# Two activations of a two-layer feed-forward kernel: parametric relu and mish as ScalarE table functions read from PSUM

## The chip, the cores and the metric

The kernel runs on one core of one Trainium2 chip. The metric is the device time of one execution in microseconds (us). Three runs of the kernel before took 880.09, 880.59 and 880.71 us; the median is 880.59.

## The reference

Packed attention (a small set of 32 queries per head draws from keys and values, and the full queries then draw from that set) is followed by two feed-forward layers. 2304 tokens (4 batches of 576), width 512, hidden width 2048, all in float32; the weights arrive as 64-bit floats.

```
x = attention(q, k, v, p)            # [2304, 512]
h = x @ w_in                         # first layer, [2304, 2048]
g = maximum(0.01 * h, h)             # leaky relu
x = g @ w_out                        # [2304, 512]
h = x @ w_in2                        # second layer
sp = where(h > 20, h, log1p(exp(minimum(h, 20))))
g = h * tanh(sp)                     # mish
out = g @ w_out2
```

## The kernel before

Products of this size carry each float32 operand as two parts: a high part, the value rounded to the type float32r, and a low part, the value less its high part. A product is then three matmuls, high x high, high x low and low x high (`PASSES`, line 20). So every block that goes into a matmul has to be made twice: rounded, and as a remainder.

**Weights** come in as 64-bit words. For each unit of 128 x 512, `convs` (line 115) puts together the float32 on VectorE in three instructions (L128, L130, L132), rounds it on ScalarE (L140) and subtracts on GpSimd (L141). The loads are issued on SyncE's queue (SP), each when the unit before it has freed its staging tile.

**First layer.** The hidden width is worked through in chunks of 128 columns, for one half batch (288 tokens, `HALF`) at a time: 128 steps, listed in `slots`. The first product is folded with the attention: `packed_w` (line 355) multiplies the packed values into the weights once for each batch and 512 columns, and ScalarE and VectorE split the result (L366, L367). A step's `l1_h` (line 373) has six matmuls of 288 columns into one of two PSUM banks of the pool `psh`, and then four instructions make the leaky relu and its two parts: a copy out of PSUM on ScalarE (L391), the relu on VectorE in place (L392), the rounding cast on ScalarE (L394), the subtraction on GpSimd (L395). `l1_y` (line 405) multiplies such a block with the output weights, twelve matmuls of 288 columns into four banks of the pool `psy` that hold a running sum over several steps. Its block is that of three steps before (`LAG`, line 663). When a sum ends, each of its four banks is copied into `yp` by ScalarE (L424) or added to it by VectorE (L426), and the next sum's first matmuls need these banks. `y_parts` (line 432) later splits the finished `yp` for the second layer (L439 on ScalarE, L441 on GpSimd).

**Attention and order.** The attention of the batches runs among these steps: `pack` and `spread` are generators that transpose, multiply, take Exps and split, and each `tick()` (line 535) advances some of them by a step. For the first layer the order of all of this is a string written out by hand (`SCHED`, line 25): each tick takes the next field and advances what its letters name (2 and 5 the attention, c the weight conversions, P the packed weights). After the string is used up, generators advance by fixed periods. Each engine works through its instructions in the order in which they were emitted.

**Second layer.** Blocks of 384 tokens (`TB`), 96 steps in the loop at line 688. `l2_h` (line 446) has twelve matmuls of 384 columns into one of three banks. `l2_g` (line 459) computes h * a / (a + 2) with a = e * (e + 2) and e = exp(min(h, 20)): VectorE clips (L463), ScalarE takes Exp (L464), VectorE makes a (L476), ScalarE takes Ln(a + 2) and the Exp of its negative (L478, L479), and in the next pass of the loop VectorE multiplies twice (L468, L469, which reads PSUM again), ScalarE rounds (L471) and GpSimd subtracts (L472). `two_c` holds the constant 2 that Ln adds. `l2_o` (line 484) takes the block of three steps before: nine matmuls of 512 columns into three banks of the pool `pso` (five banks), summed over four steps, then copied into `op` by ScalarE (L498) or added by VectorE (L500), and stored. At the start of the kernel one table set is loaded into ScalarE (L582, `natural_log_exp_and_others`).

Of the kernel before, what the change touches and what calls it, by code (L numbers as in the profile page):

```python
# [8 lines left out]
F32 = mybir.dt.float32  # L9
F32R = mybir.dt.float32r  # L10
U32 = mybir.dt.uint32
I64 = mybir.dt.int64
AF = mybir.ActivationFunctionType
ALU = mybir.AluOpType
AX = mybir.AxisListType
PSUM = bass.MemoryType.PSUM

# The large products carry a float32 operand as two float32r parts, hi = round(x)
# to 12 significant bits and lo = x - hi, and take hi*hi + hi*lo + lo*hi.
PASSES = ((0, 0), (0, 1), (1, 0))  # L20

# The order of emission: in which the first steps of the first layer's attention (0, 1, 2: pack; 3, 4, 5: spread), its packed
# queries (p), its loads and their regrouping, the first weights (C: a unit, c: a step) and products (P) start.
ORDER = "xwLPxPk0K0p01xP0x1cc0x11wxCcxxx0xxxQ1qxccw4PaC311cx3Pc40PcC4b3dcc0c31CxC40xPxxCPx13x33c3c2444c2423x34wC43x542x3x5xx434"
# [5 lines left out]
def tile_packed_attention_moe2(ctx: ExitStack, tc: tile.TileContext, q, k, v, p, w1i, w1o, w2i, w2o, out):  # L30
    nc = tc.nc
    B, H, S, D = q.shape
    NP = p.shape[2]
    NT, DM = out.shape
    DF = w1i.shape[1]
    R = 6
# [4 lines left out]
    TB = 384  # L41
# [6 lines left out]
    const = ctx.enter_context(tc.tile_pool(name="const", bufs=1))  # L48
# [3 lines left out]
    ident = const.tile([128, 128], F32, name="ident")  # L52
    two_c = const.tile([128, 1], F32, name="two_c")
    ppT = const.tile([128, B * NG, 2, 2 * NP], F32, name="ppT")
# [6 lines left out]

# [1 line left out]
    wi, wo, w2a, w2b = {}, {}, {}, {}  # L63
    w_tiles = {}

    def w_tile(kind, n):
        """The tile that the n-th group of a weight lies in, taken from the ring when first asked for."""
        if (kind, n) not in w_tiles:
            if kind == "i":
                t = wp.tile([128, 4, 512], F32, tag="A", name=f"wi{n}")  # L70
            elif kind == "o":
                t = wp.tile([128, 2, 2, 512], F32R, tag="A" if n % 4 == 2 else "B", name=f"wo{n}")
            else:
                t = wp.tile([128, 2, 2, 512], F32R, tag="A" if kind == "a" else "B", name=f"w2{kind}{n}")
            w_tiles[kind, n] = t
        return w_tiles[kind, n]
# [29 lines left out]
    def w_ahead(i):  # L106
        """Load the next unit of the weights, if it is not more than the stages allow ahead of unit i."""
        n = len(w_list_done)
        if n < len(w_list) and n <= i + (EARLY - 1 if n < 2 * EARLY else 1):
            sts[n] = w_load(w_list[n][1], n)  # L110
            w_list_done.append(n)
# [39 lines left out]

# [1 line left out]
    a2_t = {}  # L153
    packed, ready = set(), set()
# [45 lines left out]
    def spare(nm):  # L200
        """Room that the first layer's blocks take later."""
        return gp.tile([128, S], F32, tag="gx", name=nm, bufs=4)
# [10 lines left out]
    def pack(u, bank, first=False):  # L213
        """The packed queries of four heads of a batch, and the values that they draw."""
        if u == 1:
# [5 lines left out]
        if not first:  # L221
            load(k, "k", u + 1)
        # scores of the packed queries: [4 heads x NP, S]
        sc = []
        mx2 = att.tile([128, 2], F32, tag="mx2", name="mx2")
        for hb in range(2):
            ps = bank()
# [25 lines left out]
        for hb in range(2):  # L253
            ps = bank()
# [4 lines left out]
            yield  # L259
        # packed values, transposed: [2 heads x D, 4 heads x NP], the diagonal blocks kept  # L260
        ps = bank()
# [20 lines left out]
    def spread(u, bank, first=False):  # L282
        """The queries' attention over the packed keys; the first batch's in finer steps."""
        b, g = divmod(u, NG)
# [5 lines left out]
        while u not in packed:  # L290
            yield
        # scores of the queries on the packed keys, transposed: [4 heads x NP, S]
        bt = att.tile([128, S], F32, tag="sm", name="bt")
        for hb in range(2):
            ps = bank()
# [41 lines left out]

    # steps of the first layer: (pass, batch, half, chunk of 128 columns, first and last of its sum, sum's number in the pass,
    # last sum of the pass); a pass's first and last weights are used up in two sums, which leaves more time to replace them
    slots = []  # L340
# [30 lines left out]

# [1 line left out]
    def l1_h(i):  # L373
        pas, b, hb, f = slots[i][:4]
        pw = pw_t[(pas * B + b) * 2 + f % 8 // 4]
        fc = f % 4 * 128
        ps = psh.tile([128, 512], F32, tag="h", name="ps_h1")[:, :HALF]
        n = 0
        for g in range(NG):
            for x, y in PASSES:  # L380
                mm(  # L381
                    ps,
                    pw[:, g, x, fc : fc + 128],
                    a2_t[b, g][:, y, hb * HALF : (hb + 1) * HALF],
                    start=n == 0,
                    stop=n == 3 * NG - 1,
                )
                n += 1
        prog["h"] = i
        gf = gp.tile([128, HALF], F32, tag="gf", name="gf", bufs=3)  # L390
        nc.scalar.copy(gf, ps)  # L391
        nc.vector.scalar_tensor_tensor(out=gf, in0=gf, scalar=0.01, in1=gf, op0=ALU.mult, op1=ALU.max)  # L392
        gx = gp.tile([128, 2, HALF], F32R, tag="gx", name="gx", bufs=4)
        nc.scalar.copy(gx[:, 0], gf)  # L394
        nc.gpsimd.tensor_tensor(out=gx[:, 1], in0=gf, in1=gx[:, 0], op=ALU.subtract)  # L395
        return gx
# [8 lines left out]
    def l1_y(i, gx, tick):  # L405
# [3 lines left out]
        yb = ystate["b"]  # L409
        # the half's columns by blocks of the second layer: (block, first column, column in it, width)  # L410
        pieces, c = [], 0
# [32 lines left out]

# [1 line left out]
    def l2_h(s):  # L446
# [11 lines left out]

    def l2_g(ps, prev):
        # h * tanh(log(1 + e)) = h * a / (a + 2) with a = e * (e + 2); the block before is finished on the way  # L460
        if ps is not None:
            m = gp2.tile([128, TB], F32, tag="t0", name="m")
            nc.vector.tensor_scalar(m, ps, 20.0, None, ALU.min)  # L463
            nc.scalar.activation(m, m, AF.Exp)  # L464
        gx = None
        if prev is not None:
            ps0, m0, a0, r0 = prev
            nc.vector.tensor_tensor(out=a0, in0=a0, in1=r0, op=ALU.mult)  # L468
            nc.vector.tensor_tensor(out=m0, in0=ps0, in1=a0, op=ALU.mult)  # L469
            gx = gp2.tile([128, 2, TB], F32R, tag="gx", name="gx2", bufs=3)  # L470
            nc.scalar.copy(gx[:, 0], m0)  # L471
            nc.gpsimd.tensor_tensor(out=gx[:, 1], in0=m0, in1=gx[:, 0], op=ALU.subtract)  # L472
        if ps is None:
            return None, gx
        a = gp2.tile([128, TB], F32, tag="t1", name="a")
        nc.vector.scalar_tensor_tensor(out=a, in0=m, scalar=2.0, in1=m, op0=ALU.add, op1=ALU.mult)  # L476
        ln = gp2.tile([128, TB], F32, tag="t2", name="ln")
        nc.scalar.activation(ln, a, AF.Ln, bias=two_c)  # L478
        nc.scalar.activation(ln, ln, AF.Exp, scale=-1.0)  # L479
        return (ps, m, a, ln), gx  # L480

# [26 lines left out]
    def store(src, c):  # L508
        # token columns run over (batch, r, p): token p * R + r
        done = 0  # L510
        while done < 128:
            b, s = divmod(c + done, S)
            r, pp = divmod(s, SP)
            n = min(128 - done, SP - pp)
            rows = out[b * S : (b + 1) * S, :].rearrange("(p r) e -> r p e", r=R)
            nc.sync.dma_start(rows[r, pp : pp + n, :], src[done : done + n, :])
            done += n
# [39 lines left out]
    with tc.manual_schedule():  # L557
        # right side: what the first layer alone needs
        with ExitStack() as st1:
# [28 lines left out]
            for j in range(2):  # L588
                nc.sync.dma_start(praw[32 * j : 32 * j + 32, :, 64 * j : 64 * j + 64], pv[j])
            nc.gpsimd.memset(two_c, 2.0)  # L590
            nc.gpsimd.memset(ppT, 0.0)
# [94 lines left out]
        S2 = 4 * 4 * NB2  # L686
        prev, gxs = None, {}
        for s in range(S2 + 3):
            ps = None
            if s < S2:  # L690
                fc = s // (4 * NB2) * 4 + s % 4
                wait_for(lambda: fc in w2a and prog["yb"] >= min(s // 4, NB2 - 1))
                ps = l2_h(s)
            prev, gx = l2_g(ps, prev)
            if gx is not None:
                gxs[s - 1] = gx
            tick()
            if 0 <= s - 3:
                s0 = s - 3
                fc = s0 // (4 * NB2) * 4 + s0 % 4  # L700
                wait_for(lambda: fc in w2b)
                l2_o(s0, gxs.pop(s0), tick)
            tick()
# [28 lines left out]
```

## Time and profile before

The profiled execution has a span of 874.9 us from its first to its last instruction; the page gives no other time for it. The median of the timed runs is 880.59 us.

| engine | busy us | share of the span | instructions |
|---|---|---|---|
| TensorE matmul (PE) | 838.2 | 96% | 5344 |
| TensorE weight load (PEld) | 745.8 | 85% | 5344 |
| VectorE (DVE) | 563.0 | 64% | 1013 |
| ScalarE (ACT) | 430.2 | 49% | 972 |
| GpSimd (POOL) | 344.3 | 39% | 359 |

DMA moved 53.6 MB, 61 GB/s on average. In what follows, L391 is line 391 of the kernel before; `out<-in` names the tiles that an instruction writes and reads; the arrow behind a wait or an idle time names the instruction whose end released it. Shares over the whole span mix the attention, the two layers and their ends, so the windows by stage say more. The first layer's steps lie between about 46 and 459.5 us, the second layer's from there to 868 us.

### The profile page before, as it was taken

Reading aid. Unit: us, or ns where it says so; the run is one execution under the profiler, and the core shown is the slowest. Engines: PE = TensorE matmul, PEld = TensorE weight load, DVE = VectorE, ACT = ScalarE, POOL = GpSimd, SP = SyncE. Lnnn points to the kernel's source line nnn. Section 1 sums busy time; section 2 is a strip of 40 time slices with the busy share of each in tenths; the row PEclk is TensorE's granted clock in tenths of the full one; section 3 lists DMA queues with packets and bytes.
Section 4 is the critical chain, followed back from the end, with each engine's and each line's share of the span. In section 5 each row is a group of like instructions: output and inputs, shape, how many; then the busy total and the mean of one; then the engine's idle time right before and its main releaser. Section 6 shows DMA issues by size and latency. Waiting matters only on the chain.

```text
span 874.9 us, 14085 instructions
## 1 busy us (share of the span) xinstructions
PE 838.2 (96%) x5344; PEld 745.8 (85%) x5344; DVE 563.0 (64%) x1013; ACT 430.2 (49%) x972; POOL 344.3 (39%) x359
## 2 busy tenths in 40 slices
PE   8889999999999899999989899999999999999997
PEld 7767779788889889898888799988999889889996
DVE  2788644543867833237587644898669976786654
ACT  3544545454354344444435665565545554455543
POOL 1354524323435645446665322344224432232221
PEclk9999999999999999999999999999999999999999
DMA  9953323220232200001131000122001210001212
GB/s 220 316 135 79 103 60 78 55 55 1 87 108 97 97 1 1 1 2 56 42 121 49 25 1 1 48 77 69 1 25 50 72 49 1 25 25 37 72 37 73
DMA packets 52579, 53.59 MB, mean 61 GB/s; under 512 B 31264, under 2 KB 44064, under 8 KB 52512
## 3 DMA queue, kind: packets, MB, share of 16 engines
q1 hardware_dynamic: 52512, 52.70, 21.1%
q8 instruction: 42, 0.69, 0.3%
q14 instruction: 25, 0.20, 0.1%
HBM read 47.97 MB, written 4.72 MB: 60 GB/s over the span
## 4 chain that ended last, share of the span: by engine, by line
PE 71%; DVE 16%; issue 4%; ACT 3%; DMA 3%; POOL 1%; SPq 0%; ACTq 0%; POOLq 0%; DVEq 0%
PE ps_o L494 19%; PE ps_h L454 18%; PE ps_y L419 18%; PE ps_h L381 9%; DVE gf L392 3%; PE ps_pw L365 2%; DVE cv L130 2%; DMA st_q<-in_q_dram 2%; DVE a L468 2%; PE ps_a L266 2%; DVE cv L132 1%; DVE m L469 1%; PE ps_a L209 1%; DVE cv L128 1%; POOL gx L472 1%
## 5 line engine op out<-in xcount | busy, mean ns | idle before, releaser
L419 PE MATMUL ps_y<-gx,wo 128*128 128x288 f32 x1536 | 241.3, 301 | 9.4 <-DVE yp L426 5.6
L419 PEld LDWEIGHTS ps_y<-gx,wo 128*128 128x128 f32 x1536 | 213.2, 190 | 32.9 <-issue 22.4
L494 PE MATMUL ps_o<-w2b,gx 128*128 128x512 f32 x864 | 217.6, 395 | 4.6 <-ACT op L498 2.7
L454 PE MATMUL ps_h<-yh,w2a 128*128 128x384 f32 x768 | 212.0, 337 | 0.7 <-DVE m L469 0.7
L472 POOL TENSOR_TENSOR gx<-m,gx 128x384 fp32r<-128x384 f32 x96 | 100.7, 1049 | 255.7 <-ACT gx L471 241.9
L494 PEld LDWEIGHTS ps_o<-w2b,gx 128*128 128x128 f32 x864 | 160.6, 187 | 36.9 <-ACT op L498 3.2
L395 POOL TENSOR_TENSOR gx<-gf,gx 128x288 fp32r<-128x288 f32 x128 | 112.7, 880 | 188.6 <-ACT gx L394 175.4
L392 DVE SCALAR_TENSOR_TENSOR gf<-gf 128x288 f32<-128x288 f32 x128 | 81.5, 637 | 124.9 <-ACT gf L391 124.5
L454 PEld LDWEIGHTS ps_h<-yh,w2a 128*128 128x128 f32 x768 | 140.3, 188 | 5.7 <-DVE m L469 1.5
L454 PE MATMUL ps_h<-yl,w2a 128*128 128x384 f32 x384 | 128.8, 335 | 0.0
L381 PE MATMUL ps_h<-a,pw 128*128 128x288 f32 x768 | 125.1, 298 | 2.5 <-ACT pw L366 1.8
L463 DVE TENSOR_SCALAR m<-ps_h 128x384 f32<-128x384 f32 x96 | 53.2, 555 | 104.1 <-PE ps_h L454 78.9
L381 PEld LDWEIGHTS ps_h<-a,pw 128*128 128x128 f32 x768 | 108.7, 188 | 8.5 <-issue 3.8
L394 ACT CAST gx<-gf 128x288 fp32r<-128x288 f32 x128 | 55.4, 433 | 119.4 <-DVE gf L392 119.4
L464 ACT ACTIVATE m<-m 128x384 f32<-128x384 f32 x96 | 50.4, 525 | 110.6 <-DVE m L463 110.3
L471 ACT CAST gx<-m 128x384 fp32r<-128x384 f32 x96 | 49.3, 514 | 65.5 <-DVE m L469 61.9
L391 ACT COPY gf<-ps_h 128x288 f32<-128x288 f32 x128 | 51.2, 400 | 61.1 <-PE ps_h L381 59.8
L454 PEld LDWEIGHTS ps_h<-yl,w2a 128*128 128x128 f32 x384 | 72.2, 188 | 4.3
L468 DVE TENSOR_TENSOR a<-a,ln 128x384 f32<-128x384 f32 x96 | 63.5, 661 | 1.2 <-ACT ln L479 1.2
L478 ACT ACTIVATE ln<-a,two_c 128x384 f32<-128x384 f32 x96 | 58.9, 614 | 3.8 <-DVE a L476 3.8
L476 DVE SCALAR_TENSOR_TENSOR a<-m 128x384 f32<-128x384 f32 x96 | 56.2, 586 | 1.2 <-ACT m L464 1.2
L469 DVE TENSOR_TENSOR m<-ps_h,a 128x384 f32<-128x384 f32 x96 | 53.5, 557 | 3.3
(116 smaller groups left out, 825.3 us busy)
## 6 DMA issues: line engine op xcount, KB each, us to landing
st<-in_moe_w_in_dram SPq DMA_DIRECT2D x32, 512.0 KB, 3.7
st<-in_moe_w_out_dram SPq DMA_DIRECT2D x32, 512.0 KB, 3.5
raw_v<-in_v_dram SPq DMA_DIRECT2D x8, 576.0 KB, 4.9
raw_k<-in_k_dram SPq DMA_DIRECT2D x24, 144.0 KB, 3.3
raw_q<-in_q_dram SPq DMA_DIRECT2D x24, 144.0 KB, 3.3
out_dram<-op SPq DMA_DIRECT2D x12, 192.0 KB, 2.4
out_dram<-op SPq DMA_DIRECT2D x12, 128.0 KB, 2.4
st_k<-in_k_dram SPq DMA_DIRECT2D x2, 576.0 KB, 6.0
```

Source lines behind the costliest of these rows:

```text
L381: mm(ps, pw[:, g, x, fc : fc + 128], a2_t[b, g][:, y, hb * HALF : (hb + 1) * HALF], start=n == 0, stop=n == 3 * NG - 1,)
L392: nc.vector.scalar_tensor_tensor(out=gf, in0=gf, scalar=0.01, in1=gf, op0=ALU.mult, op1=ALU.max)
L394: nc.scalar.copy(gx[:, 0], gf)
L395: nc.gpsimd.tensor_tensor(out=gx[:, 1], in0=gf, in1=gx[:, 0], op=ALU.subtract)
L419: mm(yb[e][:, :HALF], wo[f][:, x, e * 128 : (e + 1) * 128], gx[:, y], start=first and n == 0, stop=last and n == 2)
L454: mm(ps, w[:, x, c, :], y2[y][:, c, :], start=n == 0, stop=n == 3 * NE - 1)
L468: nc.vector.tensor_tensor(out=a0, in0=a0, in1=r0, op=ALU.mult)
L469: nc.vector.tensor_tensor(out=m0, in0=ps0, in1=a0, op=ALU.mult)
L472: nc.gpsimd.tensor_tensor(out=gx[:, 1], in0=m0, in1=gx[:, 0], op=ALU.subtract)
L476: nc.vector.scalar_tensor_tensor(out=a, in0=m, scalar=2.0, in1=m, op0=ALU.add, op1=ALU.mult)
L478: nc.scalar.activation(ln, a, AF.Ln, bias=two_c)
L494: mm(ob[t], gx[:, x, t * 128 : (t + 1) * 128], w[:, y], start=fi == 0 and n == 0, stop=fi == 3 and n == 2)
```

## The change

`l1_h` and `l2_g` no longer build the activations from several instructions. ScalarE reads the PSUM bank twice with the function Prelu (alpha 0.01) or Mish: once with the rounded type as output, once in full float32. The low part, full less rounded, is made by VectorE, not by GpSimd. The second layer's activation is finished in the pass of the loop in which it begins, so `l2_o` follows `l2_h` by two steps; its loop has 98 passes, not 99. `two_c` and its memset go. The second layer's tiles are now `gx2` with four buffers and `gf2` with three. The load of the table set at L582 is as before, and no other is written in the code.

```diff
@@ l1_h @@
         gf = gp.tile([128, HALF], F32, tag="gf", name="gf", bufs=3)
-        nc.scalar.copy(gf, ps)
-        nc.vector.scalar_tensor_tensor(out=gf, in0=gf, scalar=0.01, in1=gf, op0=ALU.mult, op1=ALU.max)
         gx = gp.tile([128, 2, HALF], F32R, tag="gx", name="gx", bufs=4)
-        nc.scalar.copy(gx[:, 0], gf)
-        nc.gpsimd.tensor_tensor(out=gx[:, 1], in0=gf, in1=gx[:, 0], op=ALU.subtract)
+        nc.scalar.activation(gx[:, 0], ps, AF.Prelu, alpha=0.01)
+        nc.scalar.activation(gf, ps, AF.Prelu, alpha=0.01)
+        nc.vector.tensor_tensor(out=gx[:, 1], in0=gf, in1=gx[:, 0], op=ALU.subtract)
         return gx
@@ l2_g @@
-    def l2_g(ps, prev):
-        if ps is not None:
-            m = gp2.tile([128, TB], F32, tag="t0", name="m")
-            nc.vector.tensor_scalar(m, ps, 20.0, None, ALU.min)
-            nc.scalar.activation(m, m, AF.Exp)
-        gx = None
-        if prev is not None:
-            ps0, m0, a0, r0 = prev
-            nc.vector.tensor_tensor(out=a0, in0=a0, in1=r0, op=ALU.mult)
-            nc.vector.tensor_tensor(out=m0, in0=ps0, in1=a0, op=ALU.mult)
-            gx = gp2.tile([128, 2, TB], F32R, tag="gx", name="gx2", bufs=3)
-            nc.scalar.copy(gx[:, 0], m0)
-            nc.gpsimd.tensor_tensor(out=gx[:, 1], in0=m0, in1=gx[:, 0], op=ALU.subtract)
-        if ps is None:
-            return None, gx
-        a = gp2.tile([128, TB], F32, tag="t1", name="a")
-        nc.vector.scalar_tensor_tensor(out=a, in0=m, scalar=2.0, in1=m, op0=ALU.add, op1=ALU.mult)
-        ln = gp2.tile([128, TB], F32, tag="t2", name="ln")
-        nc.scalar.activation(ln, a, AF.Ln, bias=two_c)
-        nc.scalar.activation(ln, ln, AF.Exp, scale=-1.0)
-        return (ps, m, a, ln), gx
+    def l2_g(ps):
+        gx = gp2.tile([128, 2, TB], F32R, tag="gx", name="gx2", bufs=4)
+        gf = gp2.tile([128, TB], F32, tag="t0", name="gf2", bufs=3)
+        nc.scalar.activation(gx[:, 0], ps, AF.Mish)
+        nc.scalar.activation(gf, ps, AF.Mish)
+        nc.vector.tensor_tensor(out=gx[:, 1], in0=gf, in1=gx[:, 0], op=ALU.subtract)
+        return gx
@@ the second layer's loop @@
-        prev, gxs = None, {}
-        for s in range(S2 + 3):
-            ps = None
+        gxs = {}
+        for s in range(S2 + 2):
             if s < S2:
                 fc = s // (4 * NB2) * 4 + s % 4
                 wait_for(lambda: fc in w2a and prog["yb"] >= min(s // 4, NB2 - 1))
-                ps = l2_h(s)
-            prev, gx = l2_g(ps, prev)
-            if gx is not None:
-                gxs[s - 1] = gx
+                gxs[s] = l2_g(l2_h(s))
             tick()
-            if 0 <= s - 3:
-                s0 = s - 3
+            if 0 <= s - 2:
+                s0 = s - 2
```

## Rows read from the trace of the kernel before

**Rows 1.** Busy us (x instructions) of each engine by stage, clock, DMA share, GB/s
```profile
60.00:240.00 180.00, 174.09 (x1420) 147.82 (x1419) 102.72 (x197) 83.84 (x223) 69.15 (x69) 1.00 0.25 64
240.00:459.50 219.50, 210.06 (x1484) 193.30 (x1483) 126.46 (x228) 94.67 (x252) 116.99 (x137) 0.99 0.16 53
459.50:868.00 408.50, 403.12 (x2011) 361.82 (x2011) 295.20 (x506) 222.64 (x429) 137.43 (x126) 1.00 0.12 37
```

**Rows 2.** Chain of waits, second layer: start us, us, what
```profile
564.54 2.10 PE ps_o L494 x9
568.74 2.10 PE ps_o L494 x9
```

**Rows 3.** Windows around the longest wait; engines in order PE PEld DVE ACT POOL
```profile
447.70:451.10 3.40, 0.08 (x2) 0.07 (x1) 2.75 (x5) 1.05 (x3) 3.40 (x3) 1.00 0.51 154
451.10:454.50 3.40, 3.25 (x12) 2.93 (x13) 3.37 (x10) 1.37 (x4) 1.32 (x2) 0.50 0.46 139
```

**Rows 4.** What TensorE waited for, 240 to 875 us: total us, times, longest
```profile
PE ps_y L419 <- DVE yp L426: 5.6, 3, 3.3
PE ps_o L494 <- ACT op L498: 2.7, 1, 2.7
PE ps_o L494 <- DVE op L500: 1.9, 2, 1.3
PE ps_y L419 <- POOL wo L141: 1.6, 1, 1.6
PE ps_y L419 <- ACT yp L424: 1.3, 1, 1.3
PE ps_y L419 <- ACT wo L140: 0.8, 1, 0.8
PE ps_h L454 <- DVE m L469: 0.7, 2, 0.5
```

**Rows 5.** Timeline, 444 to 453 us: start us, us, instruction [idle before <-releaser]
```profile
444.40 0.96 PE L381 MATMUL ps_h<-a,pw 128*128 128x288 f32 x6
...
444.77 0.69 DVE L130 SCALAR_TENSOR_TENSOR cv<-st,cv 128x512 uint32<-128x512 uint32 x1
...
447.07 0.43 ACT L394 CAST gx<-gf 128x288 fp32r<-128x288 f32 x1 [1.91 <-DVE gf L392]
...
448.73 1.75 DVE L130 SCALAR_TENSOR_TENSOR cv<-st,cv 128x512 uint32<-128x512 uint32 x1
```

**Rows 6.** ScalarE by line: xcount | busy us, mean ns | idle before <-releasers
```profile
L394 ACT CAST gx<-gf 128x288 fp32r<-128x288 f32 x128 | 55.4, 433 | 119.4 <-DVE gf L392 119.4
L391 ACT COPY gf<-ps_h 128x288 f32<-128x288 f32 x128 | 51.2, 400 | 61.1 <-PE ps_h L381 59.8 <-POOL yl L441 1.1
...
L258 ACT COPY a<-ps_a 96x384 f32<-96x384 f32 x12 | 5.6, 472 | 0.3 <-PE ps_a L257 0.3
...
L582 ACT ACT_TABLE_LOAD x1 | 1.3, 1283 | 0.7 <-PEq L717 0.7
```

**Rows 7.** Lines 239 and 314: duration ns min/median/max, first and last start us
```profile
L239 ACT ACTIVATE e<-ps_a,nmb x12: 492/496/503, 54.2 to 193.4; 128x288 f32<-128x288 f32 x12
...
L314 ACT ACTIVATE bt<-bt x10: 435/682/697, 40.0 to 220.1; 128x576 f32<-128x576 f32 x6, 128x288 f32<-128x288 f32 x4
```

**Rows 8.** VectorE and GpSimd by line and shape: xcount | busy us, mean ns | idle
```profile
L392 DVE SCALAR_TENSOR_TENSOR gf<-gf 128x288 f32<-128x288 f32 x128 | 81.5, 637 | 124.9 <-ACT gf L391 124.5
L468 DVE TENSOR_TENSOR a<-a,ln 128x384 f32<-128x384 f32 x96 | 63.5, 661 | 1.2 <-ACT ln L479 1.2
...
L426 DVE TENSOR_TENSOR yp<-ps_y,yp 128x288 f32<-128x288 f32 x28 | 11.1, 447 | 2.1 <-PE ps_y L419 2.0
...
L395 POOL TENSOR_TENSOR gx<-gf,gx 128x288 fp32r<-128x288 f32 x128 | 112.7, 880 | 188.6 <-ACT gx L394 175.4 <-PE ps_y L419 5.5 <-issue 2.6
```

**Rows 9.** What TensorE waited for, 60 to 240 us: total us, times, longest
```profile
PE ps_a L229 <- ACT kT L210: 1.2, 1, 1.2
...
PE ps_pw L365 <- ACT kT L210: 0.6, 1, 0.6
```

More of the change, by code (lines that the diff above doesn't have):

```diff
@@ L52, in tile_packed_attention_moe2 @@
     ident = const.tile([128, 128], F32, name="ident")
-    two_c = const.tile([128, 1], F32, name="two_c")
     ppT = const.tile([128, B * NG, 2, 2 * NP], F32, name="ppT")
@@ L589, in tile_packed_attention_moe2 @@
                 nc.sync.dma_start(praw[32 * j : 32 * j + 32, :, 64 * j : 64 * j + 64], pv[j])
-            nc.gpsimd.memset(two_c, 2.0)
             nc.gpsimd.memset(ppT, 0.0)
```

## The prediction

> **What bounds the kernel now.** I read the windows by stage first, then the chain of waits, then what TensorE waited for, then the timeline around its longest wait, and last the groups by line of the engines that the change touches.
>
> The windows [rows 1] show TensorE busy for 174.09 of 180 us between 60 and 240 us, for 210.06 of 219.5 us up to the end of the first layer at 459.5 us, and for 403.12 of 408.5 us in the second layer. ScalarE, VectorE and GpSimd stand idle for 28 to 66% of these stretches. The chain shows the pace of the second layer [rows 2]: nine matmuls of `l2_o` in 2.10 us, the next nine 4.20 us after them, with `l2_h` between. 96 steps of 4.20 are 403.2 us, which is TensorE's busy time there. So TensorE sets the end, and the change neither adds nor removes a matmul. What it can win is only the time in which TensorE stands: 5.9, 9.4 and 5.4 us in the three stretches, 20.7 us in all. In the first 60 us (loads, the first attention) only a handful of steps are touched, and I count no gain there.
>
> One loss hides in busy time. Just behind the longest wait the granted clock is 0.50 for 3.4 us [rows 3], the lower of TensorE's two levels (1.2 of 2.4 GHz): half of it, 1.7 us, is lost on top. The pool of what can be won is 22.4 us.
>
> **What the waits hang on.** From 240 us on TensorE waited at ten places [rows 4]: for VectorE's adds of `yp` (5.6 us in three), ScalarE's copy into `op` (2.7), VectorE's adds into `op` (1.9), GpSimd's and ScalarE's halves of a converted weight (1.6 and 0.8), ScalarE's copy of `yp` (1.3) and the bank of `l2_h` (0.7). But for the last, these aren't activations; they are things queued behind one. The longest, 3.3 us, shows how. `l1_h` had its six matmuls from 444.40 on, but ScalarE came to its cast of the step before only at 447.07, 1.91 us of it waiting for VectorE's leaky relu [rows 5]. So it reached the copy of this step's block over 2 us late, VectorE's relu of it came later still, and behind that a weight conversion (L130) took 1.75 us where the same instruction had taken 0.69 four microseconds earlier. GpSimd was busy for all of that wait, 3.40 of 3.40 us [rows 3]. Only then came the adds that free TensorE's banks.
>
> **The change, part by part.**
>
> First layer, ScalarE: copy 0.400 and cast 0.433 us a step [rows 6] become two Prelus out of PSUM. The trace has no Prelu. From below it costs the copy of that shape out of PSUM, 0.400; from above the Exp of that shape with a pointer operand, 0.496 [rows 7]. I take 0.40, as alpha is a plain number: 0.80 us against 0.83, no change in load. What changes is that no wait stands between the two: the cast's 119.4 us of waiting for VectorE go. ScalarE is through with a step 0.8 us after its matmuls, where copy, relu (0.637) [rows 8] and cast in a row made 1.47 by their means. What is queued behind (copies of `kT`, `qT` and `yp`, casts of weights) comes earlier.
>
> First layer, VectorE and GpSimd: the relu of 0.637 us becomes a subtraction of two SBUF blocks, and the subtraction on GpSimd (0.880) goes [rows 8]. The new price lies between the 288-wide add with one PSUM operand, 0.447, and the relu's own mean; I take 0.46, near the add. It waits for both Prelus, not for one copy: it ends 0.40 + 0.40 + 0.46 = 1.26 us after the matmuls, where the relu ended after 0.40 + 0.64 = 1.04. Behind it on VectorE stand weight conversions, `pw`'s subtraction and the adds of `yp`; the last free TensorE's banks at the end of a sum, and VectorE does that for 14 sums (four chunks each: 28 adds of 288 columns, 28 pairs of 192 and 96). So the new wait costs up to 14 x 0.22 = 3.1 us. Against it stands that 1.75 us of one conversion can be 0.69. With 128 + 96 subtractions gone from GpSimd there is less for VectorE to collide with (the conversions' own low halves, `yl` and the attention's stay there, and start earlier). I count half of the 3.1 as lost, +1.5.
>
> The Trainium skill ("SBUF — State Buffer", "Who interferes with whom") has a rule that speaks against this part: a VectorE instruction with two SBUF inputs and a GpSimd instruction that reads SBUF exclude each other, and whichever starts first holds the other off to its end. The trace agrees, 1.75 against 0.69 us. The new subtraction is such an instruction, so by the rule its price is the relu's contended mean, 0.64, its end comes 0.40 us later than the relu's, and the half counted as lost is 2.8 us: the sum below would end 1.3 us higher, at 865.0. By the row, with most of GpSimd's work gone, it is 0.46, and I stay with that.
>
> Second layer: ScalarE is busy 222.64 us of 408.5 and VectorE 295.20 [rows 1]. A step's two Exps, Ln and cast become two Mishes out of PSUM. The nearest row is the copy of 96 x 384 out of PSUM, 0.472 [rows 6]; raised by 0.496/0.400 as above, 0.585. That is 0.94 to 1.17 us of a 4.20 us step; I take 0.94, and even three times that would fit. VectorE's four instructions become one, between 0.447 (the 288-wide add) and 0.661 (the 384-wide product out of SBUF) [rows 8]; I take 0.56 between them. A block of `l2_o` comes two steps behind its `l2_h`, not three: between them stand two `l2_o` and two `l2_h`, 8.4 us, and the chain needs 0.94 + 0.56. The loop has 98 passes for 99, so weights are converted a few ticks earlier against the matmuls; their loads on SP's queue follow the conversions. The bank of `l2_h` is free after the two Mishes, no longer after the next step's product. Mish needs one table load more, 1.283 us [rows 6], on a ScalarE that idles for 186 us of this stage: nothing, and 1.3 us once if it is uncovered. `two_c` and its memset on GpSimd's queue give nothing.
>
> **The sum.** Second layer: all three kinds of waits go, as their engines have under half a step's work: -5.4. From 240 us: the copy of `yp` stands behind a cast that waits for VectorE, -1.3; the weight's halves stand behind relu, cast and GpSimd's subtraction, 2.4 us down to 0.3, -2.1; of the adds of `yp`, 5.6 us, I leave 0.8 (two places, 0.4 each, about one add), -4.8, since ScalarE's lateness of 2 us and a microsecond of the conversion go; with no wait of 3.3 us the clock stays up, -1.7. From 60 to 240 us [rows 9] the waits for `kT` (1.2 and 0.6) stand behind casts that wait for VectorE, -1.8; of the other 4.1 us, the attention's own chains mostly, I take 1.3. New waits: +1.5. Together -5.4 - 1.3 - 2.1 - 4.8 - 1.7 - 3.1 + 1.5 = -16.9 us. The profiled execution's span is 874.9 us, so 858.0; the median of the runs, 880.59, lies 5.7 above that span, and with the same 5.7 I forecast 863.7 us.
>
> **The rivals.**
>
> *All waits go.* The whole pool, 22.4 us: 858.2. For it: every wait in [rows 4] is for an engine that gets lighter. Against: the attention's waits hang on its own chains.
>
> *The ends of the sums stay as they are.* VectorE's wait for the second Prelu holds the adds back by what the shorter conversions give: the 5.6 us and the 1.7 us of clock stay and 3.1 come on top. Left are 5.4 + 1.3 + 2.1 + 3.1 - 3.1 = 8.8 us of gain: 871.8. For it: the adds stand right behind the subtraction. Against: the long wait had a contended conversion in it, and a ScalarE that was late.
>
> *The tables switch, and it is slower.* If Prelu isn't in the loaded set with Exp, each group of Exps between two steps costs two loads, 2 x 1.283 = 2.57 us of ScalarE. `pack`'s twelve Exps among the steps come in six pairs up to 193 us, `spread`'s six full-width ones singly up to 220 us [rows 7]: at most 12 groups, 30.8 us. If all of it lands on TensorE, 863.7 + 30.8 = 894.5; it is slower than before from the seventh group on that lands there. For it: no row shows which functions share a set. Against: one load in the whole trace serves Copy, Cast, Exp and Ln [rows 6], the change leaves that line (L582) alone, and ScalarE's slack would hide a part. The Trainium skill ("ScalarE: Activation LUTs", "Table sets: the hidden batching unit") says that cheap functions such as relu and copy stand in every set, without naming Prelu, and puts a switch at about 2.7 us, load and drain; by it 12 groups would be some 64 us, an estimate from that page.
>
> *It doesn't do what it says:* a Prelu or Mish that runs as more than one pass. At twice the price ScalarE has 1.6 us a step in the first layer, under the 2.36 of a step's 18 matmuls (5184 columns at the pace of [rows 2], 4608 in 2.10); this falls into the second rival.
>
> **How the numbers follow.** Forecast 0.66 (859 to 870), all waits 0.10, ends of sums 0.14 (0.02 of it within no change), tables 0.10 (0.07 slower, 0.03 about even). A measurement here can tell about 0.2%, 1.8 us. Faster 0.66 + 0.10 + 0.12 = 0.88, same 0.02 + 0.03 = 0.05, slower 0.07. The range, 857 to 875, takes in the first three cases.
>
> **What would show it.** Right: steps of 4.20 us in the second layer without a wait of TensorE; no stretch at clock 0.50 near the end of the first layer; the Prelus without idle time for VectorE; L130 and L132 near 0.69 us on average; one table load more. Wrong: over three table loads; TensorE waiting at the adds of `yp` in more than three places; a Prelu above 0.5 us or a Mish above 0.7; a new wait of `l1_h` or `l2_h` for a bank that ScalarE still reads.

## The result and the profile after

The changed kernel takes 854.11 us (median of four runs, 853.08 to 854.52), the kernel before 880.43 in the same session: a ratio of 0.970, interval 0.9686 to 0.9714. It is 26.3 us faster; 16.9 were forecast, and the time lies 2.9 us under the range.

The windows of the changed kernel by stage, engines in the order PE PEld DVE ACT POOL, then clock, DMA share and GB/s. The second layer now begins at 443.4 us:

```profile
60.00:240.00 180.00, 177.11 (x1455) 152.65 (x1454) 96.67 (x203) 85.26 (x235) 28.32 (x22) 1.00 0.27 68
240.00:443.40 203.40, 202.28 (x1439) 186.40 (x1438) 106.18 (x218) 85.29 (x239) 48.10 (x59) 1.00 0.15 50
443.40:844.80 401.40, 401.40 (x2013) 362.73 (x2012) 127.72 (x219) 107.80 (x238) 36.89 (x30) 1.00 0.13 39
```

Against [rows 1], TensorE's idle time has gone from 5.9 to 2.9, from 9.4 to 1.1 and from 5.4 to 0 us. In the second layer the engines beside it do half or less of what they did, and it runs without a pause.

All that TensorE waited for from 60 us to the end (total us, times, longest), after; it answers to [rows 4] and [rows 9]:

```profile
PE ps_a L208 <- ACT e L238: 1.2, 1, 1.2
PE ps_y L417 <- DVE yp L424: 1.1, 2, 0.7
PE ps_h L380 <- POOL a L330: 0.6, 1, 0.6
PE ps_a L208 <- DVE pw L366: 0.6, 1, 0.6
PE ps_a L208 <- ACT kT L209: 0.5, 1, 0.5
```

Of the eleven waits that [rows 4] count from 240 us on (the prediction says ten), two short ones at the adds of `yp` are left. The new instructions, ScalarE's groups by line (xcount | busy us, mean ns | idle before and who ended it):

```profile
L391 ACT ACTIVATE gx<-ps_h 128x288 fp32r<-128x288 f32 x128 | 52.6, 411 | 129.2 <-PE ps_h L380 129.1
L392 ACT ACTIVATE gf<-ps_h 128x288 f32<-128x288 f32 x128 | 52.2, 408 | 0.0
L461 ACT ACTIVATE gx<-ps_h 128x384 fp32r<-128x384 f32 x96 | 47.1, 491 | 269.3 <-PE ps_h L452 269.3
...
L566 ACT ACT_TABLE_LOAD x1 | 1.3, 1283 | 0.7 <-PEq L696 0.7
L461 ACT ACT_TABLE_LOAD x1 | 1.3, 1283 | 0.0
```

and VectorE's by line and shape:

```profile
L393 DVE TENSOR_TENSOR gx<-gf,gx 128x288 fp32r<-128x288 f32 x128 | 69.7, 544 | 144.9 <-ACT gf L392 144.2
L463 DVE TENSOR_TENSOR gx<-gf,gx 128x384 fp32r<-128x384 f32 x96 | 54.2, 565 | 269.2 <-ACT gf L462 269.2
L129 DVE SCALAR_TENSOR_TENSOR cv<-st,cv 128x512 uint32<-128x512 uint32 x48 | 40.1, 835 | 1.1
L131 DVE SCALAR_TENSOR_TENSOR cv<-st,cv 128x512 uint32<-128x512 uint32 x48 | 34.5, 719 | 1.0
```

Prelu costs 0.41 us (0.40 taken), Mish 0.49 (0.47), the subtractions 0.54 and 0.57 (0.46 and 0.56). One table load was added, and none between Exp and Prelu: the third rival is out. In the steps ScalarE waits only for TensorE now (before, 119.4 us for VectorE [rows 6]).

**Where the 26.3 us lie.** TensorE runs the 3328 matmuls ahead of the second layer in the same order in both kernels, so the start of one and the same matmul can be compared, and the lead grows where a wait went. The table takes the profiled executions, 874.9 and 852.0 us of span, and then what lies between span and median (5.6 us before, 2.1 after).

| step of the sum | forecast | measured |
|---|---|---|
| first 60 us | 0 | -1.1 |
| 60 to 240 us | -3.1 | -4.5 |
| copy of `yp` at 241 us | -1.3 | -1.5 |
| weight halves at 300 us | -2.1 | -2.7 |
| adds of `yp` at 419 and 451 us | -4.8 | -5.0 |
| clock, and the small rest of the first layer | -1.7 | -1.1 |
| second layer, first to last matmul (409.7 to 402.3 us) | -5.4 | -7.4 |
| after the last matmul | 0 | +0.4 |
| VectorE's new wait | +1.5 | 0 |
| **span** | **-16.9** | **-22.9** |
| from span to the median of the runs | 0 | -3.5 |
| **median** (rounded rows) | **-16.9** | **-26.3** |

How a wait is longer than its idle time, at the copy of `yp`. TensorE's timeline before (start us, us), then after:

```profile
239.18 0.95 PE L381 MATMUL ps_h<-a,pw 128*128 128x288 f32 x6
241.44 1.73 PE L419 MATMUL ps_y<-gx,wo 128*128 128x288 f32 x11 [1.30 <-ACT yp L424]
```

```profile
233.52 0.96 PE L380 MATMUL ps_h<-a,pw 128*128 128x288 f32 x6
234.31 1.76 PE L417 MATMUL ps_y<-gx,wo 128*128 128x288 f32 x12
```

From the first to the second start it is 2.26 us before and 0.79 after: 1.47 us gone where the profile showed 1.30 of idle. Unhindered, the next matmul starts while the last still counts as busy (0.79 against 0.96), and the first 0.17 us of a wait is in that.

### The profile page after: what moved, and what is told of

Same layout as the page of the kernel before. It is cut to its first block, busy times and chain, and to the rows that moved or that the text cites. A ratio compares the mean times of both kernels' runs of the same rounds, so it can differ in the third digit from the quotient of the medians.

```text
span 852.0 us, 13012 instructions
## 1 busy us (share of the span) xinstructions
PE 832.2 (98%) x5344; PEld 745.4 (87%) x5344; DVE 369.3 (43%) x725; ACT 308.5 (36%) x781; POOL 131.2 (15%) x134
## 4 chain that ended last, share of the span: by engine, by line
PE 91%; DVE 4%; DMA 2%; ACT 1%; issue 1%; SPq 0%; POOL 0%; ACTq 0%; DVEq 0%; POOLq 0%
PE ps_h L452 24%; PE ps_o L478 23%; PE ps_y L417 23%; PE ps_h L380 11%; PE ps_pw L364 3%; DMA st_q<-in_q_dram 2%; PE ps_a L265 2%; PE ps_a L208 1%; PE ps_a L296 1%; PE ps_a L228 1%; PE ps_a L256 0%; DVE cv L129 0%; DVE cv L127 0%; DVE cv L131 0%; DVE gx L393 0%
## 5 line engine op out<-in xcount | busy, mean ns | idle before, releaser
L463 DVE TENSOR_TENSOR gx<-gf,gx 128x384 fp32r<-128x384 f32 x96 | 54.2, 565 | 269.2 <-ACT gf L462 269.2
L461 ACT ACTIVATE gx<-ps_h 128x384 fp32r<-128x384 f32 x96 | 47.1, 491 | 269.3 <-PE ps_h L452 269.3
L393 DVE TENSOR_TENSOR gx<-gf,gx 128x288 fp32r<-128x288 f32 x128 | 69.7, 544 | 144.9 <-ACT gf L392 144.2
L391 ACT ACTIVATE gx<-ps_h 128x288 fp32r<-128x288 f32 x128 | 52.6, 411 | 129.2 <-PE ps_h L380 129.1
L140 POOL TENSOR_TENSOR w2a<-cv,w2a 128x512 fp32r<-128x512 f32 x16 | 21.9, 1370 | 226.4 <-ACT w2a L139 226.4
L392 ACT ACTIVATE gf<-ps_h 128x288 f32<-128x288 f32 x128 | 52.2, 408 | 0.0
L462 ACT ACTIVATE gf<-ps_h 128x384 f32<-128x384 f32 x96 | 46.5, 484 | 0.0
L439 POOL TENSOR_TENSOR yl<-yp,yh 128x288 fp32r<-128x288 f32 (+2 forms) x48 | 31.9, 690 | 83.3 <-ACT yh L437 82.9
L129 DVE SCALAR_TENSOR_TENSOR cv<-st,cv 128x512 uint32<-128x512 uint32 x48 | 40.1, 835 | 1.1
L484 DVE TENSOR_TENSOR op<-ps_o,op 128x512 f32<-128x512 f32 x54 | 34.5, 683 | 3.5 <-PE ps_o L478 3.5
L131 DVE SCALAR_TENSOR_TENSOR cv<-st,cv 128x512 uint32<-128x512 uint32 x48 | 34.5, 719 | 1.0
```

What stands on the lines that cost most here:

```text
L129: nc.vector.scalar_tensor_tensor(out=d, in0=hi, scalar=0xC0000000, in1=d, op0=ALU.bitwise_and, op1=ALU.bitwise_or)
L140: nc.gpsimd.tensor_tensor(out=t[:, j, 1], in0=x, in1=t[:, j, 0], op=ALU.subtract)
L391: nc.scalar.activation(gx[:, 0], ps, AF.Prelu, alpha=0.01)
L392: nc.scalar.activation(gf, ps, AF.Prelu, alpha=0.01)
L393: nc.vector.tensor_tensor(out=gx[:, 1], in0=gf, in1=gx[:, 0], op=ALU.subtract)
L461: nc.scalar.activation(gx[:, 0], ps, AF.Mish)
```

## The experiments

Every one gives its median beside the kernel before, run on the same chip: 880.4 us in the first four, 880.5 in the next four, 880.9 in the last four.

**e0, the kernel before, unchanged.**

> The kernel before, unchanged, for its span and its time in the same run. The forecast took 5.7 us to lie outside the span (880.59 less the profile's 874.9); of the changed kernel every run has 1.8 to 1.9 us there. Theory A: the profiled execution of before was a shorter one than the timed runs. Then spans here are 878 to 879 us for times of 880 to 881, 1.9 outside, and the change's gain inside the span is 26, not 23 us. Rival B: what lies outside differs between the two programs. Then the spans are 874.5 to 875.5 us with 5 to 6 us outside.

Theory A holds. In all ten runs 1.8 us lie outside the span, as for the changed kernel (1.8 to 1.9), so nothing outside the span was won. Spans run from 877.3 to 881.7 us, and the time goes roughly with the mean granted clock: 879.1 and 880.3 us at 0.992, 879.1 to 881.1 at 0.990, 883.5 at 0.983. The profile that the forecast started from is at 0.996 and 874.9 us. Of the 43 runs of this kernel in the three sessions of experiments (e0's ten among them) one was at 0.996, and it took 876.7 us, the fastest of all. What differs are, for a good part, stretches at the lower level behind the waits. Windows of e0, behind its waits at 419 and 453 us (columns as above, the clock after the fifth engine):

```profile
420.30:423.70 3.40, 3.40 (x17) 3.40 (x16) 0.77 (x2) 1.07 (x5) 2.30 (x5) 0.54 0.33 129
454.40:457.80 3.40, 3.40 (x15) 3.40 (x16) 3.33 (x8) 1.99 (x9) 2.47 (x3) 0.54 0.49 154
```

Only the second of these stretches is in the profile that the prediction read [rows 3]. Behind its own wait at 419 us that profile shows the upper level, and 27 matmuls where e0 shows 17:

```profile
419.60:423.00 3.40, 3.40 (x27) 3.40 (x27) 1.31 (x3) 1.92 (x8) 2.54 (x6) 1.00 0.31 123
```

Matmul by matmul, e0's span is 2.5 us longer: 0.7 arises in the first 26 us, 1.5 at the stretch of 420 us and 0.3 around the one of 454 us. The changed kernel's profile has neither stretch (its clock is 1.00 in all three windows above); where TensorE waited 2.1 and 3.3 us it now waits 0.0 and 0.7.

**e1 and e2, one layer at a time.** `l1_h` as changed with the old second layer; the old `l1_h` with the second layer as changed.

> The change in the first layer alone (two Prelus, low part on VectorE), the second layer as before. Theory: the two halves of the gain add up, since TensorE is in order and each wait that went belongs to one layer; by the two traces 15.9 us of the gain lie before the second layer's first product. So 862 to 865 us, and 7 to 10 us remain for the second layer. Rival: the halves share a cause (GpSimd's load, weights that come late), and one alone gives much less than its part: 867 us or more.

> The change in the second layer alone (two Mishes, low part on VectorE, two steps of distance), the first layer as before. Theory: its part of the gain, 7.4 us by the traces and up to 10 with what is not yet placed: 870 to 873 us, one table load more. Rival: 876 us or more, because the second layer's waits come from lateness handed over by the first.

862.45 us (861.95 to 863.41; 0.979) and 872.58 (870.75 to 873.4; 0.990). 17.9 and 7.8 us, together 25.7 of 26.3: the halves add up.

**e3, low parts back on GpSimd**, in both layers.

```diff
-        nc.vector.tensor_tensor(out=gx[:, 1], in0=gf, in1=gx[:, 0], op=ALU.subtract)
+        nc.gpsimd.tensor_tensor(out=gx[:, 1], in0=gf, in1=gx[:, 0], op=ALU.subtract)
```

> The changed kernel with the low parts of both layers back on GpSimd. Theory: most of the gain is that ScalarE no longer waits for VectorE between its two instructions; that stays, so 855 to 860 us, with a few us lost where VectorE's weight conversions collide with GpSimd again (L129 and L131 back to about 1.0 and 0.9 us). Rival: the gain is that GpSimd's subtractions went; then over half of the 26 us are lost, 867 us or more.

852.02 us (851.67 to 852.82; 0.967, interval 0.9651 to 0.9697): nothing is lost. Yet the collisions are back, VectorE by line and shape in e3:

```profile
L131 DVE SCALAR_TENSOR_TENSOR cv<-st,cv 128x512 uint32<-128x512 uint32 x48 | 47.9, 999 | 1.4
L129 DVE SCALAR_TENSOR_TENSOR cv<-st,cv 128x512 uint32<-128x512 uint32 x48 | 44.7, 931 | 1.4
```

TensorE's wait for the adds of `yp` is 1.0 us all the same. In e3 no part of a step's activation stands on VectorE, so nothing in its queue waits for ScalarE's part of a step. From the first to the last matmul of the second layer e3 takes 402.3 us, as the changed kernel does. It is also the fastest version run, 2 us under the changed kernel (853.99 in the last session, as e14). No run of the one overlaps one of the other, but the intervals of the ratios do.

**e4, the low parts on VectorE alone.** The kernel before with this exchange in both layers:

```diff
-        nc.gpsimd.tensor_tensor(out=gx[:, 1], in0=gf, in1=gx[:, 0], op=ALU.subtract)
+        nc.vector.tensor_tensor(out=gx[:, 1], in0=gf, in1=gx[:, 0], op=ALU.subtract)
```

> The kernel before with one part of the change alone: the low parts of both layers on VectorE, not on GpSimd; copy, relu, cast and the chain of Exps and Ln stay. Theory: GpSimd's subtractions were not what cost the time (without the table functions VectorE's queue only gets longer), so no gain: 878 to 890 us, though L130 and L132 drop below 0.9 us. Rival: the collisions with GpSimd were the cause; then 866 to 872 us.

930.58 us (929.74 to 930.84; 1.058): 50 us slower, far beyond what either theory gave. What VectorE waited for in e4, its four longest:

```profile
DVE gf L392 <- ACT gf L391: 76.0, 77, 2.9
DVE gx L472 <- ACT gx L471: 63.6, 96, 1.4
DVE gx L395 <- ACT gx L394: 62.5, 125, 0.6
DVE a L468 <- ACT ln L479: 29.9, 46, 1.2
```

The subtraction waits for a cast that waits for VectorE's own relu or product (ScalarE's cast waits 130.6 us for the relu here): the two queues hold each other up twice a step, and what stands behind (adds of `yp` and `op`) makes TensorE wait 12.7 and 11.7 us. Collisions with GpSimd are not what costs here: 8 of the 128 weight conversions (L130, L132) take over 1 us, where 45 did before. So the part of the change that looks like a mere exchange of engines costs 50 us with the old instructions in their old order. With the table functions it gains nothing (e3), and with the old instructions in another order it gains 7 us (e13 against e10).

**e5 and e7, two details.** The changed kernel with `l2_o` three steps behind; and with one table pass from PSUM and then a cast (in both layers):

```diff
-        nc.scalar.activation(gx[:, 0], ps, AF.Prelu, alpha=0.01)
         nc.scalar.activation(gf, ps, AF.Prelu, alpha=0.01)
+        nc.scalar.copy(gx[:, 0], gf)
```

> The changed kernel with l2_o three steps behind l2_h, as before, not two. Theory: the distance has no part in the gain, as the chain of two Mishes and a subtraction takes 1.6 us of 8.4: 853 to 856 us. Rival: the shorter distance lets weights and banks come free earlier and is worth 2 us or more: 856 us or more.

> The changed kernel with one table function out of PSUM and a plain cast of its result for the rounded part, so that PSUM is read once. Theory: what counts is that both instructions stand on ScalarE with nothing of VectorE between them; the second read of PSUM is only another way to that: 852 to 856 us. Rival: the second pass from PSUM itself matters (an earlier start, or a bank held longer): a difference of 3 us or more from 854.

854.18 us (853.57 to 855.4) and 854.52 (853.49 to 854.79). Neither the distance nor the second read of PSUM has a part in the gain that these runs can tell.

**e10, the old instructions, the cast one step later.** In `l1_h` of the kernel before:

```diff
         nc.vector.scalar_tensor_tensor(out=gf, in0=gf, scalar=0.01, in1=gf, op0=ALU.mult, op1=ALU.max)
-        gx = gp.tile([128, 2, HALF], F32R, tag="gx", name="gx", bufs=4)
-        nc.scalar.copy(gx[:, 0], gf)
-        nc.gpsimd.tensor_tensor(out=gx[:, 1], in0=gf, in1=gx[:, 0], op=ALU.subtract)
-        return gx
+        finish_g()
+        late.append((i, gf))
```

`finish_g` (left out here) makes the cast and the subtraction of the step before.

> The kernel before with its old instructions, no Prelu and no Mish, but the first layer's rounding cast and GpSimd's subtraction of a step issued behind the next step's copy, so that ScalarE's cast finds VectorE's relu done. Theory: the first layer lost its time by ScalarE's waiting inside a step; this alone brings most of what the first layer's change gave (880.4 to 862.5): 863 to 869 us, with the cast's 119 us of waiting down to a third or less. Rival: the relu's price on VectorE (0.64 us) or GpSimd's collisions were the cause, which stay here: 874 us or more.

875.28 us (875.02 to 877.17; 0.995): 5.2 us of the first layer's 17.9. The theory falls. ScalarE's cast hardly waits any more, in e10 by line:

```profile
L402 ACT CAST gx<-gf 128x288 fp32r<-128x288 f32 x128 | 55.9, 436 | 3.2 <-DVE gf L392 3.1
```

The two waits for `kT` that the prediction names (1.2 and 0.6) and the one for the copy of `yp` at 241 us go, as the prediction had it. But the adds of `yp` still take 4.2 us and the weight's halves 2.3, and a wait of the attention for an Exp is 2.1 us where it was 0.6. From e10's list of what TensorE waited for, 60 to 460 us:

```profile
PE ps_y L427 <- DVE yp L434: 4.2, 3, 2.6
PE ps_a L209 <- ACT e L239: 2.1, 1, 2.1
...
PE ps_y L427 <- POOL wo L141: 1.6, 2, 0.8
...
PE ps_y L427 <- ACT wo L140: 0.7, 2, 0.4
```

This profile is of e10's slowest run, and with its new wait 5.2 us is rather the least that ScalarE's lateness is worth.

**e12 and e13, GpSimd's subtractions by themselves.** e12 is the changed kernel with GpSimd's old load put back as work that nobody reads; e13 is e10 with the low part on VectorE.

```diff
         nc.vector.tensor_tensor(out=gx[:, 1], in0=gf, in1=gx[:, 0], op=ALU.subtract)
+        nc.gpsimd.tensor_tensor(out=gf, in0=gf, in1=gx[:, 0], op=ALU.subtract)
```

> The changed kernel with 128 subtractions more on GpSimd, one a step of the first layer behind VectorE's, whose result nobody reads: GpSimd's old load is back, the rest is as changed. e10 left 13 us of the first layer's gain away although ScalarE no longer waited. Theory: there VectorE stood in the step's chain and collided with GpSimd as well, and both together kept its adds of yp and its conversions late. Then this kernel, with VectorE in the chain and collisions, loses a good part: 858 to 866 us, TensorE's wait for the adds of yp at 3 us or more. Rival: it was the relu's own time on VectorE; then 853 to 856 us.

> e10 with the first layer's low part on VectorE, not GpSimd (also one step later): old instructions, ScalarE doesn't wait, no collisions with GpSimd's subtractions, but 0.64 us of relu and 0.46 of subtraction a step on VectorE. Theory of collisions: better than e10's 875.3, 864 to 870 us. Rival, VectorE's time in the queue: no better or worse than e10, 875 us or more.

e12: 863.53 us (862.11 to 864.12; 0.980), 9.5 above the changed kernel on the same chip. Nothing else was touched, and Prelu's two groups are as in the changed kernel (0.412 and 0.407 us). VectorE's timeline in e12 ahead of the last sum's end (start us, us):

```profile
442.20 0.46 DVE L393 TENSOR_TENSOR gx<-gf,gx 128x288 fp32r<-128x288 f32 x1 [0.59 <-ACT gf L392]
442.57 1.75 DVE L129 SCALAR_TENSOR_TENSOR cv<-st,cv 128x512 uint32<-128x512 uint32 x1
444.25 0.51 DVE L425 TENSOR_TENSOR yp<-ps_y,yp 128x192 f32<-128x192 f32 x2
```

It is the picture of [rows 5]: the step's instruction, a conversion of 1.75 us, and only then the adds. What TensorE waited for from 240 us on in e12:

```profile
PE ps_y L418 <- DVE yp L425: 4.4, 4, 2.1
PE ps_y L418 <- POOL wo L140: 1.7, 2, 1.4
```

These are the two kinds that e10 kept. They aren't all of it: of the 10 us between the two profiles about 3 arise before 240 us, in the loads and the attention. e13 took 868.23 us (865.36 to 869.99; 0.986), 7.1 less than e10, though VectorE does more in it. From its list, 60 to 449 us:

```profile
PE ps_y L427 <- DVE yp L434: 3.2, 3, 2.0
...
PE ps_y L427 <- POOL wo L141: 0.8, 1, 0.8
```

Both sides agree: while VectorE stands in the step's chain, GpSimd's subtractions cost 7 to 10 us. They slow VectorE's instructions, and they stand ahead of GpSimd's other work (the weights' low halves, the attention's products); no run separates these two ways.

**e9 and e14.** e9 is e3 with the later batches' subtraction and product of the attention on VectorE (`PERIODS` with 'svssvvgvgv'); e14 is the changed kernel once more.

> A version that could beat the changed kernel: as e3 (low parts on GpSimd, 852.0 there) with the later batches' subtraction and product of the attention's second softmax on VectorE, which has no part in the steps any more, not GpSimd. If TensorE's waits for the attention (about 2 us between 60 and 120 us) are GpSimd's slow instructions, 849 to 851.5 us; if not, 851.5 to 853.

> The changed kernel, unchanged, on the chip of this job, to stand beside e9 and e12: 853 to 855 us, and 1.8 us outside the span in every run, as for the kernel before.

854.42 us (852.68 to 857.14) and 853.99 (853.72 to 855.09). e9 lies above what either case gave and brings nothing over e3, and the changed kernel comes out as before.

## Why the prediction was wrong

Right were the direction, TensorE as what sets the end, the prices of Prelu, Mish and the second layer's subtraction, one table load that costs nothing, the steps of the second layer without a wait, and which waits go. TensorE's idle time fell by 16.9 us (span less busy: 36.7 to 19.8), where the forecast's waits, the new one set against them, make 15.2. Wrong were two other things.

Of the 9.6 us between forecast and measurement the first of them makes some 4 and the second some 6.

**The step that failed first** is the last of the sum: "the median of the runs, 880.59, lies 5.7 above that span, and with the same 5.7 I forecast 863.7 us". Of the 5.7 only 1.8 lie outside the span (e0). The other 3.9 were the profiled execution's own luck (the table has 3.5 of it, by the medians 880.43 and 854.11): it ran at a mean clock of 0.996 where 32 of the 43 runs are at 0.989 to 0.992, having one half-clock stretch fewer at least, at the wait of 419 us. That stretch, 1.5 us in e0, hangs on a wait that the change removes, so it is gain and not a constant. Another 0.7 is a difference of the first 26 us, and 0.3 arises around the wait of 451 us. The other 1.4 no trace shows; that they are more such stretches is argued from the runs' clocks. With 1.8 the same sum gives 859.8.

**The second** is the size of the pool: "What it can win is only the time in which TensorE stands", 20.7 us and 1.7 of clock. The span fell by 22.9 us, 6.0 more than the sum. The table says where: 2.0 more in the second layer, 1.5 of new wait that did not come, 1.4 more from 60 to 240 us, 1.0 more in the three rows behind it, and 1.1 in the first 60 us, which the prediction put at nothing (two profiles of the kernel before differ by 0.7 there); 0.6 of clock and 0.4 at the end go the other way. Busy time fell by 6.0 us (838.2 to 832.2), not by 1.7, with as many matmuls, and this is where the pool was too small.

A wait of 288-column matmuls is 0.15 to 0.17 us longer than the idle time that the profile shows; of the 24 waits of over 0.2 us ahead of the second layer eleven went. In the second layer all five went, and the excess between the starts of neighbouring matmuls makes 6.7 us there where the waits add up to 5.3 [rows 4]; 0.7 of its 7.4 is a slightly closer pace, whose reason no run shows. With the clock these are some 5 of the 6 us (an estimate); the rest isn't placed. The clock term itself was too large: from the start at 452.26 us to the second layer's first matmul it is 7.06 us before and 6.14 after, 0.9 us and not 1.7.

**VectorE's new wait cost nothing**, against +1.5. It waits 144.2 us for ScalarE in all, more than the 124.5 us of the relu [rows 8], and yet TensorE's wait for the adds of `yp` is 1.1 us, where e3, without VectorE in the step, has 1.0.

**Of the mechanism half was right.** The prediction named two things ahead of the adds of `yp`, a ScalarE that is late and a contended conversion, and gave no share to either. Taking ScalarE's lateness away by itself brings 5.2 us of the first layer's 17.9 (e10). Of the other 12.7, 7 to 10 us need two things at once: an instruction of the step in VectorE's queue, and GpSimd's subtractions beside it. The changed kernel removes the second, e3 the first, and both have the whole gain; with both there, 9.5 us of it are lost (e12). The conversions didn't have to fall to 0.69 us, as the last part of the prediction wanted: they are at 0.84 and 0.72 in the changed kernel and at 0.93 and 1.00 in e3.

The conversions' slowness itself the traces show directly: in the kernel before, the 33 of 128 (L130 and L132) during which GpSimd did nothing took 0.69 us at most, and the 49 that began inside an instruction of GpSimd took 1.35 on average and 1.81 at most. With the step's subtractions gone from GpSimd, twelve of 128 began so. The rule of the Trainium skill ("SBUF — State Buffer", "Who interferes with whom"), that a VectorE instruction with two SBUF inputs and a GpSimd instruction that reads SBUF exclude each other, was weighed in the prediction and set aside by the nearest row; these conversions agree with it. For the new subtraction the mean is 0.54 us, between the row's 0.46 and the rule's 0.64.

What stays open: why e3 is about 2 us faster than the changed kernel (most of its lead arises between 54 and 82 us, in the attention), how the rest of e13's distance to e1 (868.2 to 862.5) divides between the relu's time and its wait, and which of the instructions that left ScalarE and VectorE freed the second layer of its waits (e3, e5 and e7 rule out GpSimd's subtraction, the distance and the second read).

## What to carry to other kernels

Before a profile's span is used as the base of a sum, compare its mean clock and its own time with those of the other runs: a stretch of half clock behind a wait is part of what removing the wait gives, whether this execution had it or not. Where an in-order engine serves both the steps and the jobs that free buffers, ask of every instruction of the step what it waits for and what it can collide with; here a step's instruction on VectorE and GpSimd's subtractions could each stay alone, and both together cost 7 to 10 us. An edit that only changes engines can cost 50 us, nothing, or gain 7 (e4, e3, e13), depending on whether the instruction ahead of it waits for the same engine.

## What the runs showed of the hardware that was not expected

The same kernel took 876.7 to 884.2 us in 43 runs, and its time followed the mean granted clock, loosely, from 0.996 to 0.983 (the 17 runs at 0.990 took 878.5 to 881.4), while the changed kernel in eight runs kept to 853.1 to 855.1 at 0.993 to 0.997. Prelu and Mish out of PSUM cost about what a copy does, 0.41 and 0.49 us against 0.40 (the same shape) and 0.47 (96 x 384), and rounding on the way out costs next to nothing (411 against 408 ns).
